# Two-layer ReLU² network behind block attention: where the block sums of the squares and of the weights are formed, in which order their products run, and how the softmax steps are laid between them

## The chip, the cores and the metric

One core of one Trainium2 chip runs the whole program. The metric is the time of one execution in microseconds; three executions of the kernel before gave a median of 700.97 us (700.53 to 701.24). Engines are named as in the profile: PE multiplies matrices, PEld loads its weights, DVE is VectorE, ACT is ScalarE, POOL is GpSimd, SP issues the DMAs.

## The reference

Attention over 4 batches, 8 heads, 768 positions and 64 channels gives 3072 rows of 512, which go through `h = relu(x @ w_in)` (512 to 2048) and `(h * h) @ w_out` (2048 to 512). In the attention, each query sees its neighbours within 15 positions and one summary of every block of 32 keys:

```python
k_sum = k.reshape(B, H, nb, block, D).max(axis=3)
v_sum = v.reshape(B, H, nb, block, D).mean(axis=3)
scores_l = scale * q @ k.T            # masked to |i - j| < 16
scores_s = scale * q @ k_sum.T + log(block)
a = softmax(concat(scores_l, scores_s))
attn = a @ concat(v, v_sum)
h = relu(x @ w_in)
out = (h * h) @ w_out
```

## The kernel before

The 3072 rows are 12 chunks of 256 rows (two groups of 128). Every operand of a large multiplication is split into a high and a low part, and three products (high·high, high·low, low·high) stand for one. Chunks 0 and 1 run in an opening stage that an order written out by hand sets (`START`), beside the loading and decoding of the weights. From chunk 2 on the program is a loop: chunk c has eight slots, and slot n handles the n-th pair p of the sixteen 128-wide blocks of the hidden layer. Nothing reorders it: each engine takes its instructions in the order in which the code issues them.

In slot n the PE runs the first layer of pair n (24 matmuls, L388), and then the second layer of the pair before it, n − 1. From chunk 3 on, for seven of the eight pairs, the second layer is not the plain 2 by 2 product of blocks (12 matmuls of 512 columns, L580) but seven products of sums of blocks (Strassen's way, 21 matmuls of 256 columns, L515). That needs sums of the blocks of the squares, for each slot, and sums of the weights' blocks, once for each pair.

The squares of a slot (`squares_and_sums`, L431): ACT takes the ReLU from the accumulator `ph` into `r` (L396) and the high part of the square of three plain blocks into `gh` (L402); DVE multiplies `ph` by `r` in place (L436) and subtracts for the plain low parts `gl` (L437); POOL forms four sums in place in `r`, each 128x128 (L439 to L442); then ACT rounds the four sums to their high parts (`split_sums`, L446) and POOL subtracts for their low parts (L447). `r` has two buffers, which alternate. The products (`products`, L505) go block by block: for every one of the seven, both uses of the high part and then the low part.

The sums of the weights (`build`, L474) have five steps: 0 and 1 add high and low parts of the two blocks' halves on POOL (L480), 2 and 3 are four subtractions on POOL (L483 to L488), and 4 rounds on ACT (L492, L493) and takes the low parts on DVE (L494, L495). The table `BUILDS` says in which slot of chunk 2 or 3 and at which place in it each step stands: steps 0 to 3 of a pair stand together at a slot's end, and step 4 ahead of the next slot's ReLU. Four of the seven pairs' sums are written to memory and streamed back in each chunk (`stream`).

Beside this, chunk c prepares the attention of the two groups a = 2c + 2 and a + 1 of the next chunk: scores on PE (L273, in slots 0 and 3), a masked maximum for each head on DVE (L300), the exponential on ACT (L308), the inverse of the sums on DVE (L318, L321), the normalizing on POOL (L326, four heads at a time), twelve 32-row transposes on DVE (L339, three, five and four in three places), and in slot 7 the weighted values on PE (L357), whose result is split on ACT and DVE (L370, L373) into the input of the next chunk. For the next batch's block summaries, half a key or value array at a time is loaded into the one buffer `kv_sb` (L188) and reduced on DVE (L191, L196); a load follows at a slot's end, and its reduction one slot later. `place_k` and `place_v` copy summaries to where the multiplications read them. `period` hands each slot its steps in three lists: "before" the squares, "after" them (but ahead of `split_sums`), and "last". In slot 0 the results of the chunk before are added up and stored (L544 to L556).

Of the kernel before, what the change touches and what calls it, by code (L numbers as in the profile page):

```python
# [76 lines left out]
def attn_ffn_kernel(ctx: ExitStack, tc: tile.TileContext, q, k, kt, v, vt, v0, w, masks, ident, mean, out):  # L77
# [346 lines left out]
    def squares(ph, k):  # L424

        r = relu(ph, r_sb[:, k], nc.scalar)
        high_square(flat(gh_sb, k), r)
        square(ph, r)
        low_square(flat(gl_sb, k), ph, flat(gh_sb, k))

    def squares_and_sums(ph, k):  # L431
# [5 lines left out]
        nc.vector.tensor_sub(out=gl_sb[:, k, o], in0=r[:, o], in1=gh_sb[:, k, o].bitcast(F32))  # L437
# [1 line left out]
        nc.gpsimd.tensor_sub(out=a11, in0=a11, in1=a21)  # L439
        nc.gpsimd.tensor_add(out=a21, in0=a21, in1=a22)  # L440
# [1 line left out]
        nc.gpsimd.tensor_sub(out=a12, in0=a12, in1=a22)  # L442

    def split_sums(k):
        o = slice(3 * P, 7 * P)
        nc.scalar.copy(out=gh_sb[:, k, o], in_=r_sb[:, k])  # L446
        nc.gpsimd.tensor_sub(out=gl_sb[:, k, o], in0=r_sb[:, k], in1=gh_sb[:, k, o].bitcast(F32))  # L447
# [26 lines left out]
    def build(p, step):  # L474
# [7 lines left out]
        if step == 2:  # L482
            nc.gpsimd.tensor_sub(out=t1, in0=t3, in1=t1)  # L483
# [21 lines left out]
    def products(p, k, closes):  # L505
# [4 lines left out]
        for blk, b, n_ps, o in (  # L510
            (2, b11, 2, lo), (0, b21, 6, lo), (1, t4, 7, lo),
            (5, t3, 3, lo), (6, t1, 3, hi), (4, t2, 2, hi), (3, b22, 6, hi),
        ):
            for n, (g_, w) in enumerate(((gh_sb, 0), (gh_sb, 1), (gl_sb, 0))):
                nc.tensor.matmul(  # L515
                    bank[n_ps][:, o], lhsT=g_[:, k, blk * P : (blk + 1) * P], rhs=b[:, w],
                    start=False, stop=(n == 2 and (n_ps, o.start) in closes),
                )
# [334 lines left out]
```

## Time and profile before

| what | value |
|---|---|
| median of three executions | 700.97 us |
| profiled execution, its own time | 701.86 us |
| its span, first to last instruction | 700.1 us |
| mean granted TensorE clock | 0.958 |
| PE busy (matmuls) | 620.0 us, 89% |
| DVE busy | 431.8 us, 62% |
| ACT busy | 293.1 us, 42% |
| POOL busy | 327.4 us, 47% |
| DMA, mean | 130 GB/s |

A matmul's end in the profile is modelled, so that PE counts as busy in nearly every stretch in which matmuls follow one another; the pace is better read from how many matmuls start in a stretch. "Granted clock" is the share of its full clock that the PE had. "idle before, releaser" in a row is the time that an engine stood idle ahead of its instructions, and the engine and line whose end released them. All of this is of the one profiled execution.

### The profile page before, as it was taken

The numbers are of one execution on the slowest core, as the hardware profiler recorded it, in microseconds if no ns is written. First come the engines' busy times: TensorE is split into PE (matmuls) and PEld (weight loads), VectorE is DVE, ScalarE is ACT, GpSimd is POOL, SyncE is SP. The second block draws the span as 40 slices with busy tenths as digits, with TensorE's granted clock in tenths as the row PEclk, the third lists the DMA queues.
The fourth block names the chain that finished last, engine by engine and source line by source line (L and its number), as shares of the span: only waits on it lengthen the run. The fifth ranks groups of instructions, "written<-read, shape, count | busy, mean of one in ns | idle before, by whom it ended". The sixth has DMA issues, their size and how long they took to land.

```text
span 700.1 us, 14848 instructions
## 1 busy us (share of the span) xinstructions
PE 620.0 (89%) x5859; PEld 576.2 (82%) x5859; DVE 431.8 (62%) x1112; ACT 293.1 (42%) x748; POOL 327.4 (47%) x441
## 2 busy tenths in 40 slices
...
GB/s 344 212 324 382 65 61 111 197 93 83 45 46 188 129 105 47 240 138 47 159 128 47 146 167 111 144 151 129 91 114 108 93 134 128 107 64 88 160 53 31
DMA packets 27638, 91.15 MB, mean 130 GB/s; under 512 B 3376, under 2 KB 3504, under 8 KB 25520
## 3 DMA queue, kind: packets, MB, share of 16 engines
...
q14 instruction: 24, 0.20, 0.1%
...
## 4 chain that ended last, share of the span: by engine, by line
PE 40%; DVE 18%; POOL 17%; ACT 15%; issue 4%; DMA 3%; SPq 0%; POOLq 0%; DVEq 0%; ACTq 0%
PE ph L388 16%; PE zw L515 7%; ACT e_sb L308 5%; PE o_ps L456 4%; POOL gl L447 3%; PE o_ps L515 3%; DVE r L436 3%; DVE gl L437 3%; ACT r L396 3%; ACT gh L402 3%; ACT gh L446 2%; DMA kv_sb<-in_kt 2%; POOL r L442 2%; POOL r L439 2%; POOL r L440 2%
## 5 line engine op out<-in xcount | busy, mean ns | idle before, releaser
L388 PE MATMUL ph<-xh,w_sb 128*128 128x256 f32 x1408 | 254.9, 283 | 1.4 <-DVE gl L410 1.1
L388 PEld LDWEIGHTS ph<-xh,w_sb 128*128 128x128 f32 x1408 | 219.1, 192 | 7.0 <-issue 3.0
L388 PE MATMUL ph<-xl,w_sb 128*128 128x256 f32 x704 | 198.0, 281 | 0.0
L388 PEld LDWEIGHTS ph<-xl,w_sb 128*128 128x128 f32 x704 | 134.7, 191 | 0.4 <-DVE xl L373 0.4
L308 ACT ACTIVATE e_sb<-e_sb,nmx 128x120 f32<-128x120 f32 x192 | 73.9, 386 | 90.3 <-DVE nmx L300 90.3
L446 ACT CAST gh<-r 128x512 fp32r<-128x512 f32 x63 | 39.1, 620 | 170.8 <-POOL r L442 163.7
L439 POOL TENSOR_TENSOR r<-r 128x128 f32<-128x128 f32 x63 | 29.0, 460 | 169.6 <-DVE sm L318 85.5
L436 DVE TENSOR_TENSOR r<-ph,r 128x512 f32<-128x512 f32 x63 | 43.6, 692 | 104.4 <-ACT gh L402 102.6
L339 DVE STREAM_TRANSPOSE pT<-e_sb 32x256 f32<-32x256 f32 x228 | 99.4, 436 | 5.9 <-POOL e_sb L326 2.6
L447 POOL TENSOR_TENSOR gl<-r,gh 128x512 fp32r<-128x512 f32 x63 | 80.7, 1281 | 32.9 <-ACT gh L446 32.9
L396 ACT ACTIVATE r<-ph 128x512 f32<-128x512 f32 x85 | 50.0, 588 | 44.7 <-PE ph L388 41.1
L326 POOL TENSOR_TENSOR e_sb<-e_sb,sm 128x480 f32<-128x480 f32 x43 | 44.2, 1027 | 42.6 <-DVE sm L321 19.2
L515 PE MATMUL zw<-sums,gl 128*128 128x256 f32 x126 | 40.4, 321 | 26.4 <-POOL gl L447 26.4
L402 ACT ACTIVATE gh<-r 128x384 fp32r<-128x384 f32 (+1 forms) x96 | 53.9, 561 | 20.5 <-PE o_ps L456 12.9
L515 PE MATMUL zw<-sums,gh 128*128 128x256 f32 x252 | 52.1, 289 | 8.2 <-ACT gh L446 8.0
L515 PE MATMUL zw<-w_sb,gh 128*128 128x256 f32 x252 | 52.3, 289 | 3.0 <-ACT gh L402 3.0
L580 PE MATMUL o_ps<-w_sb,gh 128*128 128x512 f32 x144 | 48.3, 419 | 6.8 <-ACT gh L402 6.8
L515 PEld LDWEIGHTS zw<-sums,gl 128*128 128x128 f32 x126 | 25.0, 198 | 33.2 <-POOL gl L447 33.2
L252 POOL TENSOR_TENSOR w_raw<-w_raw 128x1024 int32<-128x1024 int32 x16 | 34.2, 2145 | 37.3 <-ACT w_raw L243 12.5
L515 PE MATMUL o_ps<-w_sb,gh 128*128 128x256 f32 x252 | 51.0, 284 | 0.0
L515 PEld LDWEIGHTS zw<-sums,gh 128*128 128x128 f32 x252 | 39.8, 195 | 9.6 <-ACT gh L446 9.6
L300 DVE CUSTOM_DVE_ANT_0 e_sb<-s_ps,mask_sb 128x120 f32<-128x120 f32 x192 | 43.2, 274 | 6.3 <-PE s_ps L288 5.6
(120 smaller groups left out, 1211.2 us busy)
## 6 DMA issues: line engine op xcount, KB each, us to landing
sums<-sums SPq DMA_DIRECT2D x40, 768.0 KB, 4.4
...
v_sb<-in_v SPq DMA_DIRECT2D x24, 384.0 KB, 6.9
k_sb<-in_k SPq DMA_DIRECT2D x18, 384.0 KB, 5.1
...
kv<-in_kt SPq DMA_DIRECT2D x8, 384.0 KB, 3.3
kv_sb<-in_kt SPq DMA_DIRECT2D x8, 384.0 KB, 5.9
```

What stands on the lines that cost most here:

```text
L300: nc.vector.tensor_tensor_reduce(out=e_sb[:, h, 0:NK], in0=s_ps[g][h % 2][:, h // 2, 0:NK], in1=m, scale=-scale, scalar=3.0e38, op0=ALU.ad ...
L308: nc.scalar.activation(e, e, AF.Exp, bias=nmx[half][:, i : i + 1], scale=-1.0, accum_out=sm[half][:, i : i + 1])
L326: eng.tensor_mul(out=e, in0=e, in1=sm[half].unsqueeze(2).to_broadcast([P, 4, NK]))
L339: nc.vector.transpose(out=pT[g % 2][j * 32 : j * 32 + 32, :, i * 32 : i * 32 + 32], in_=e_sb[i * 32 : i * 32 + 32, :, j * 32 : j * 32 + 32],)
L388: nc.tensor.matmul(ph, lhsT=w_sb[f][:, w, cc * P : (cc + 1) * P], rhs=x[c][:, cc, :], start=(n == 0), stop=(n == 3 * NC4 - 1))
L396: nc.scalar.activation(r, ph, AF.Relu)
L402: nc.scalar.activation(gh, r, AF.Square)
L436: nc.vector.tensor_mul(out=r, in0=ph, in1=r)
L446: nc.scalar.copy(out=gh_sb[:, k, o], in_=r_sb[:, k])
L447: nc.gpsimd.tensor_sub(out=gl_sb[:, k, o], in0=r_sb[:, k], in1=gh_sb[:, k, o].bitcast(F32))
L515: nc.tensor.matmul(bank[n_ps][:, o], lhsT=g_[:, k, blk * P : (blk + 1) * P], rhs=b[:, w], start=False, stop=(n == 2 and (n_ps, o.start) in ...
L580: nc.tensor.matmul((X, Y)[tt], lhsT=g_[tt], rhs=w_sb[2 * p + i][:, w, DM:], start=(begins and i == 0 and m == 0), stop=(ends and i == 1 an ...
```

## The change

It has these parts.

1. `squares_and_sums`: the four sums move from POOL to DVE, into a tile of their own (`s`), with other signs; two of them are one instruction of 256 elements (one operand read twice), the other two follow, each needing the one before. The plain low parts (384 elements) move from DVE to POOL. `r` and `s` have one buffer each.
2. `products`: the three plain blocks come first with all three uses; then the four sums' blocks with their two uses of the high part; then the four uses of the low part.
3. `BUILDS`: the steps stand one or two at a place, over two slots for a pair; step 4 stands mostly behind the slot's squares. Signs follow part 1.
4. `period` and `slot`: a fourth list, "mid", between the squares and `split_sums`; "after" now comes behind `split_sums`. Four maxima stand together ahead of the squares, four exponentials, the inverse and the normalizing in "mid", the other four maxima and exponentials in "after"; the transposes are split six, two and four.
5. Loads of half key or value arrays have two slots instead of one until their reduction, and are spread over the chunk; the copies of `place_k` stand together in slot 7, and those of `place_v` one slot later.
6. `evict_products` and `evict_outputs` are one, and store the first half earlier.

The diff, cut to its core:

```diff
@@ BUILDS
-    2: [(p + 1, "last", p, step) for p in (1, 2, 3, 4, 5) for step in range(4)]
-    + [(p + 2, "before", p, 4) for p in (1, 2, 3, 4, 5)],
...
+    2: [(2, "a", 1, 0), (2, "a", 1, 1), (3, "b", 1, 2), (3, "b", 1, 3), (3, "a", 1, 4)]
+    + [(4, "b", 2, 0), (4, "b", 2, 1), (4, "a", 2, 2), (4, "a", 2, 3), (5, "b", 2, 4)]
...
@@ squares_and_sums
-        nc.vector.tensor_sub(out=gl_sb[:, k, o], in0=r[:, o], in1=gh_sb[:, k, o].bitcast(F32))
         a12, a22, a11, a21 = (r[:, i * P : (i + 1) * P] for i in range(4))
-        nc.gpsimd.tensor_sub(out=a11, in0=a11, in1=a21)
-        nc.gpsimd.tensor_add(out=a21, in0=a21, in1=a22)
-        nc.gpsimd.tensor_sub(out=a22, in0=a22, in1=a11)
-        nc.gpsimd.tensor_sub(out=a12, in0=a12, in1=a22)
+        s1, s3, s2, s4 = (s_sb[:, i * P : (i + 1) * P] for i in range(4))
+        nc.vector.tensor_sub(
+            out=s_sb[:, 0 : 2 * P].rearrange("p (a b) -> p a b", a=2), in0=a21.unsqueeze(1).to_broadcast([P, 2, P]),
+            in1=r[:, P : 3 * P].rearrange("p (a b) -> p a b", a=2),
+        )
+        nc.gpsimd.tensor_sub(out=gl_sb[:, k, o], in0=r[:, o], in1=gh_sb[:, k, o].bitcast(F32))
+        nc.vector.tensor_sub(out=s2, in0=a11, in1=s1)
+        nc.vector.tensor_sub(out=s4, in0=a12, in1=s2)
@@ products
-            for n, (g_, w) in enumerate(((gh_sb, 0), (gh_sb, 1), (gl_sb, 0))):
...
+        passes = [(m, n) for m in plain for n in range(3)] + [(m, n) for m in summed for n in range(2)]
+        for (blk, b, n_ps, o), n in passes + [(m, 2) for m in summed]:
@@ slot
-        for do in after:
+        for do in mid:
             do()
         if summed:
             split_sums(k)
+        for do in after:
+            do()
@@ period
-            before[n].append(lambda g=g: softmax(g, 0, 4))
-            after[n] += [lambda: inverse(0), lambda: norm(0, nc.gpsimd), lambda g=g: softmax(g, 4, 6)]
-            before[n + 1] += [lambda g=g: softmax(g, 6, 8), lambda: inverse(1), lambda: norm(1, nc.gpsimd)]
-            after[n + 1].append(lambda g=g: turn(g, 0, 3))
-            before[n + 2].append(lambda g=g: turn(g, 3, 8))
+            before[n].append(lambda g=g: [mask_max(g, h) for h in range(4)])
+            mid[n] += [lambda: [exponentials(h) for h in range(4)], lambda: inverse(0), lambda: norm(0, nc.gpsimd)]
+            after[n].append(lambda g=g: [mask_max(g, h) for h in range(4, 8)])
+            after[n].append(lambda: [exponentials(h) for h in range(4, 8)])
+            before[n + 1] += [lambda: inverse(1), lambda: norm(1, nc.gpsimd)]
+            after[n + 1].append(lambda g=g: turn(g, 0, 6))
+            before[n + 2].append(lambda g=g: turn(g, 6, 8))
...
-            for n, p in enumerate(((0, 1), (2, 3))[t // 4]):
-                last[2 * n].append(lambda p=p: load_half(b + 1, p, kt))
-                after[2 * n + 1].append(lambda p=p: sum_k(b + 1, p))
...
+            last[1].append(lambda: load_half(b + 1, p, kt))
+            after[3].append(lambda: sum_k(b + 1, p))
...
```

Line numbers of the changed kernel are four to eight higher than before. Three places show how the order on an engine moves.

On the DVE, before, from the second inverse of a chunk's second softmax (slot 5) to the last of its transposes (slot 6); `r` are the squares, `pT` the transposed probabilities:

```order
L318 SCALAR_TENSOR_TENSOR sm<-sm 128x4
L321 RECIPROCAL sm<-sm 128x4
L436 TENSOR_TENSOR r<-ph,r 128x512
L437 TENSOR_TENSOR gl<-r,gh 128x384
L339 STREAM_TRANSPOSE pT_77<-e_sb 32x8x32 x8
L436 TENSOR_TENSOR r<-ph,r 128x512
L437 TENSOR_TENSOR gl<-r,gh 128x384
L339 STREAM_TRANSPOSE pT_77<-e_sb 32x8x32 x4
```

The same place after the change, from the reciprocal on (`s` are the sums):

```order
L325 RECIPROCAL sm<-sm 128x4
L440 TENSOR_TENSOR r<-ph,r 128x512
L443 TENSOR_TENSOR s<-r 128x256
L448 TENSOR_TENSOR s<-r,s 128x128
L449 TENSOR_TENSOR s<-r,s 128x128
L343 STREAM_TRANSPOSE pT_77<-e_sb 32x8x32 x8
L440 TENSOR_TENSOR r<-ph,r 128x512
L443 TENSOR_TENSOR s<-r 128x256
L448 TENSOR_TENSOR s<-r,s 128x128
L449 TENSOR_TENSOR s<-r,s 128x128
L343 STREAM_TRANSPOSE pT_77<-e_sb 32x8x32 x4
```

In each slot one subtraction of 384 elements has given way to three instructions that form the sums; the transposes stand behind them.

On the PE, before, the last twelve of the 21 products of a slot, those of the blocks of sums (`gh` and `gl` are high and low parts; `zw` and `o_ps` the output banks; `sums` and `w_sb` the weights' side):

```order
L515 MATMUL zw<-sums,gh 128x256 x2
L515 MATMUL zw<-sums,gl 128x256
L515 MATMUL zw<-w_sb,gh 128x256 x2
L515 MATMUL zw<-w_sb,gl 128x256
L515 MATMUL zw<-sums,gh 128x256 x2
L515 MATMUL zw<-sums,gl 128x256
L515 MATMUL o_ps<-w_sb,gh 128x256 x2
L515 MATMUL o_ps<-w_sb,gl 128x256
```

The same twelve after the change:

```order
L522 MATMUL zw<-sums,gh 128x256 x2
L522 MATMUL zw<-w_sb,gh 128x256 x2
L522 MATMUL zw<-sums,gh 128x256 x2
L522 MATMUL o_ps<-w_sb,gh 128x256 x2
L522 MATMUL zw<-sums,gl 128x256
L522 MATMUL zw<-w_sb,gl 128x256
L522 MATMUL zw<-sums,gl 128x256
L522 MATMUL o_ps<-w_sb,gl 128x256
```

The sums' first low part is read by the 18th product instead of the 12th, and the first high part by the 10th as before.

On ACT, before, in slots 3 and 4 of chunk 2, where step 4 of two weights' sums stands (the casts to `sums` and `w_sb`):

```order
L492 CAST sums<-ob 128x768
L493 CAST w_sb<-ob 128x256
L396 ACTIVATE r<-ph 128x512
L402 ACTIVATE gh<-r 128x512
L492 CAST sums<-ob 128x768
L493 CAST w_sb<-ob 128x256
L308 ACTIVATE e_sb,sm<-e_sb,nmx 128x120 x4
L396 ACTIVATE r<-ph 128x512
L402 ACTIVATE gh<-r 128x512
```

After the change, from the squares of slot 3 to the second of these steps:

```order
L400 ACTIVATE r<-ph 128x512
L406 ACTIVATE gh<-r 128x512
L499 CAST sums<-ob 128x768
L500 CAST w_sb<-ob 128x256
L400 ACTIVATE r<-ph 128x512
L406 ACTIVATE gh<-r 128x512
L312 ACTIVATE e_sb,sm<-e_sb,nmx 128x120 x8
L499 CAST sums<-ob 128x768
L500 CAST w_sb<-ob 128x256
```

The ReLU and the square of slot 3 have moved ahead of the rounding of the first weights' sum. The second has moved from ahead of slot 4's ReLU to ahead of slot 5's, behind all eight exponentials.

More of the change, by code (lines that the diff above doesn't have):

```diff
@@ L39 @@
 BUILDS = {
-    2: [(p + 1, "last", p, step) for p in (1, 2, 3, 4, 5) for step in range(4)]
-    + [(p + 2, "before", p, 4) for p in (1, 2, 3, 4, 5)],
-    3: [(0, "last", 7, step) for step in range(4)] + [(1, "before", 7, 4)]
-    + [(step + 1, "after", 6, step) for step in range(4)] + [(5, "before", 6, 4)],
[7 rows of a table added]
 }
@@ L509, in products @@
         lo, hi = slice(0, CT), slice(CT, DM)
[L510 to L513, printed above, removed]
-            for n, (g_, w) in enumerate(((gh_sb, 0), (gh_sb, 1), (gl_sb, 0))):
[L515 to L518, printed above, removed]
+        plain = (2, b11, 2, lo), (0, b21, 6, lo), (1, t4, 7, lo)
+        summed = (4, t3, 3, lo), (3, t1, 3, hi), (5, t2, 2, hi), (6, b22, 6, hi)
+        passes = [(m, n) for m in plain for n in range(3)] + [(m, n) for m in summed for n in range(2)]
+        for (blk, b, n_ps, o), n in passes + [(m, 2) for m in summed]:
+            g_, w = ((gh_sb, 0), (gh_sb, 1), (gl_sb, 0))[n]
+            nc.tensor.matmul(
+                bank[n_ps][:, o], lhsT=g_[:, k, blk * P : (blk + 1) * P], rhs=b[:, w],
+                start=False, stop=(n == 2 and (n_ps, o.start) in closes),
+            )
     def open_banks(*banks):
@@ L583, in second, with slot @@
                     )
-    def slot(c, n, before, after, last):
+    def slot(c, n, before, mid, after, last):
         p, k = order(c)[n], n % 2
@@ L621, in period @@
     def period(c):
-        before, after, last = [[] for _ in range(8)], [[] for _ in range(8)], [[] for _ in range(8)]
+        before, mid, after, last = steps = [[[] for _ in range(8)] for _ in range(4)]
         for n, where, p, step in BUILDS.get(c, ()):
-            {"before": before, "after": after, "last": last}[where][n].append(lambda p=p, step=step: build(p, step))
+            steps["bmal".index(where)][n].append(lambda p=p, step=step: build(p, step))
         if c > 2:
@@ L639, in period @@
         if a >= n_g:
-            return before, after, last
+            return steps
+        if t == 0 and b:
+            after[1].append(lambda: sum_v(b, 3))
+            after[2] += [lambda: place_v(a), lambda: place_v(a + 1)]
+        elif t == 4 and b + 1 < B:
+            after[1].append(lambda: sum_v(b + 1, 1))
         if a > FROM_PAIRS:
             last[0] += [lambda: load_v(a), lambda: load_v(a + 1)]
-        if b and t == 0:
-            after[1] += [lambda: place_v(a), lambda: place_v(a + 1)]
@@ L652, in period @@
         if b + 1 < B and t:
[L653 to L657 removed]
+            p = t - 2
+            last[1].append(lambda: load_half(b + 1, p, kt))
+            after[3].append(lambda: sum_k(b + 1, p))
@@ L658, in period @@
+            last[3].append(lambda: load_half(b + 1, p, vt))
+            after[5].append(lambda: sum_v(b + 1, p))
+            last[5].append(lambda: load_half(b + 1, p + 1, kt))
+            after[7].append(lambda: sum_k(b + 1, p + 1))
+            last[7].append(lambda: load_half(b + 1, p + 1, vt))
         if a + 3 < n_g:
```

48 lines of the change are left out of this document (23 added, 25 removed), and 5 rows, old and new, of the table BUILDS.

## The prediction

> **What bounds the kernel now.** I read the page first, then the windows by chunk, the groups, the waits, and the timeline of slots that run late. The page says that the PE is the engine to watch:
>
> ```profile
> PE 620.0 (89%) x5859; PEld 576.2 (82%) x5859; DVE 431.8 (62%) x1112; ACT 293.1 (42%) x748; POOL 327.4 (47%) x441
> ```
>
> The next rows are the windows from the start of one chunk's first layer to the next: chunk 2, chunk 3 and so on to chunk 11. The columns are the stretch, its length, busy time and count of PE, PEld, DVE, ACT and POOL, the granted clock, and DMA.
>
> ```profile
> 140.97:207.09 66.12, 54.04 (x388) 46.82 (x385) 37.49 (x101) 22.93 (x62) 32.77 (x37) 0.90 0.20 70
> 207.09:272.41 65.32, 54.06 (x474) 50.09 (x473) 35.55 (x93) 23.90 (x64) 35.07 (x50) 0.90 0.38 126
> 272.41:328.23 55.82, 50.38 (x484) 47.51 (x482) 33.74 (x94) 21.46 (x60) 25.61 (x40) 0.97 0.40 133
> 328.23:381.56 53.33, 49.42 (x484) 47.26 (x483) 32.03 (x92) 21.15 (x60) 27.62 (x43) 0.97 0.33 110
> 381.56:437.43 55.87, 50.42 (x484) 47.54 (x482) 33.68 (x94) 21.47 (x60) 25.61 (x40) 0.97 0.41 133
> 437.43:494.06 56.63, 51.30 (x483) 48.44 (x482) 33.67 (x94) 21.47 (x60) 25.60 (x40) 0.94 0.40 131
> 494.06:547.34 53.28, 49.36 (x483) 47.21 (x482) 31.99 (x92) 21.14 (x60) 27.59 (x43) 0.97 0.34 109
> 547.34:597.79 50.45, 48.13 (x483) 45.96 (x482) 30.50 (x88) 21.27 (x60) 25.63 (x40) 1.00 0.35 116
> 597.79:648.34 50.55, 48.27 (x484) 46.09 (x483) 30.49 (x88) 20.78 (x58) 25.64 (x40) 1.00 0.28 90
> 648.34:700.06 51.72, 46.84 (x378) 44.99 (x376) 15.94 (x28) 14.44 (x26) 23.43 (x37) 0.99 0.22 82
> ```
>
> What would a chunk take if the PE never waited? These stretches hold, undisturbed: both groups' weighted values, a first layer, the 21 products, one group's scores, the opening of banks, and a plain second layer.
>
> ```profile
> 432.84:434.85 2.01, 2.01 (x65) 1.94 (x65) 0.67 (x1) 1.65 (x3) 0.98 (x1) 1.00 0.17 70
> 437.43:440.16 2.73, 2.73 (x26) 2.73 (x25) 0.00 (x0) 0.62 (x1) 1.55 (x2) 1.00 0.00 0
> 440.16:442.63 2.47, 2.47 (x23) 2.35 (x21) 1.39 (x2) 1.46 (x3) 0.00 (x0) 1.00 0.00 0
> 442.63:443.62 0.99, 0.99 (x34) 0.83 (x33) 0.78 (x2) 0.14 (x1) 0.00 (x0) 1.00 0.03 8
> 446.45:446.89 0.44, 0.44 (x5) 0.39 (x3) 0.23 (x4) 0.44 (x5) 0.00 (x0) 1.00 1.02 391
> 446.89:449.69 2.80, 2.80 (x14) 2.27 (x13) 0.80 (x2) 1.84 (x7) 0.00 (x0) 1.00 1.00 305
> ```
>
> A chunk with sums is 8 x 2.73 + 7 x 2.47 + 2.80 + 0.44 + 2 x 0.99 + 2.01 = 46.4 us; chunk 2, whose second layers are all plain and which has one set of scores, is 8 x (2.73 + 2.80) + 0.99 + 2.01 = 47.2. So chunks 2 and 3 lose 19 us each, chunks 4 to 8 (which load for the next batch) 7 to 10, chunks 9 and 10 about 4. The groups say to whom:
>
> ```profile
> L515 PE MATMUL zw<-sums,gl 128*128 128x256 f32 x126 | 40.4, 321 | 26.4 <-POOL gl L447 26.4
> L447 POOL TENSOR_TENSOR gl<-r,gh 128x512 fp32r<-128x512 f32 x63 | 80.7, 1281 | 32.9 <-ACT gh L446 32.9
> L439 POOL TENSOR_TENSOR r<-r 128x128 f32<-128x128 f32 x63 | 29.0, 460 | 169.6 <-DVE sm L318 85.5 <-DVE gl L437 70.1 <-ACT xh L370 14.1
> L440 POOL TENSOR_TENSOR r<-r 128x128 f32<-128x128 f32 x63 | 29.0, 460 | 4.9
> L446 ACT CAST gh<-r 128x512 fp32r<-128x512 f32 x63 | 39.1, 620 | 170.8 <-POOL r L442 163.7 <-DVE vsum L196 7.1
> L436 DVE TENSOR_TENSOR r<-ph,r 128x512 f32<-128x512 f32 x63 | 43.6, 692 | 104.4 <-ACT gh L402 102.6 <-PE ph L388 0.7
> L437 DVE TENSOR_TENSOR gl<-r,gh 128x384 fp32r<-128x384 f32 x63 | 36.7, 582 | 2.1
> L396 ACT ACTIVATE r<-ph 128x512 f32<-128x512 f32 x85 | 50.0, 588 | 44.7 <-PE ph L388 41.1 <-DVE zw L407 3.5
> L402 ACT ACTIVATE gh<-r 128x384 fp32r<-128x384 f32 (+1 forms) x96 | 53.9, 561 | 20.5 <-PE o_ps L456 12.9 <-DVE r L398 5.0
> L339 DVE STREAM_TRANSPOSE pT<-e_sb 32x256 f32<-32x256 f32 x228 | 99.4, 436 | 5.9 <-POOL e_sb L326 2.6
> L480 POOL TENSOR_TENSOR ob<-w_sb 128x512 f32<-128x512 f32 x14 | 18.0, 1300 | 16.6 <-DMA out<-ob 12.1 <-DVE w_sb L495 4.5
> L483 POOL TENSOR_TENSOR ob<-ob 128x256 f32<-128x256 f32 x7 | 5.1, 734 | 0.0
> L492 ACT CAST sums<-ob 128x768 fp32r<-128x768 f32 x7 | 5.8, 833 | 36.9 <-POOL ob L488 36.9
> L495 DVE TENSOR_TENSOR w_sb<-ob,w_sb 128x256 fp32r<-128x256 f32 x2 | 0.8, 415 | 0.0
> L191 DVE TENSOR_REDUCE ksum<-kv_sb 128x24 f32<-128x768 f32 x8 | 7.6, 953 | 14.8 <-DMA kv_sb<-in_kt 14.7
> L308 ACT ACTIVATE e_sb<-e_sb,nmx 128x120 f32<-128x120 f32 x192 | 73.9, 386 | 90.3 <-DVE nmx L300 90.3
> ```
>
> The PE's largest wait is for the sums' low parts on POOL. Three more chains feed it: ACT stands 36.9 us at L492 for the weights' sums, with the next ReLU queued behind; DVE stands 14.7 us at L191 for a load, with the next slot's multiply behind; and after a long wait the clock drops. Two windows around such a wait in chunk 6 show the last (here PE alone):
>
> ```profile
> 408.70:412.10 3.40, 3.36 (x30) 0.50 0.19 73
> 412.10:415.50 3.40, 3.40 (x45) 1.00 0.26 77
> ```
>
> 30 matmuls against 45 in the same time: such a window costs up to half of itself, 1.7 us.
>
> **Products and sums.** Take t = 0 at a slot's ReLU. Before: ReLU 0.59 and square 0.56, multiply from 1.2 to 1.9, low part 0.58 to 2.5, four POOL sums of 0.46, each 0.08 behind the last (L440's idle 4.9 over 63), to 4.7, rounding 0.62 to 5.35, low part 1.28 to 6.7. The PE meanwhile does 2.47 + 2.73, begun 0.2 ahead of the ReLU, and opens this slot's products at 5.0; the 12th of them wants the low part 1.3 later, at 6.3. The wait of 0.4 is what 26.4 us over 63 slots make. After: the paired sum costs 0.42 (L495, 256 elements), the single ones 0.25 each by the slope from 256 to 384 elements (L495 to L437): the sums end at 2.9 if nothing disturbs them. The plain low part on POOL is 1.0 (between L439's 0.46 for 128 and L447's 1.28 for 512). Does it disturb them? These rows say yes:
>
> ```profile
> 457.57 0.16 DVE L318 SCALAR_TENSOR_TENSOR sm<-sm 128x4 f32<-128x4 f32 x1 [0.73 <-ACT e_sb L308]
> 477.97 1.28 POOL L447 TENSOR_TENSOR gl<-r,gh 128x512 fp32r<-128x512 f32 x1
> 478.52 0.74 DVE L318 SCALAR_TENSOR_TENSOR sm<-sm 128x4 f32<-128x4 f32 x1 [1.54 <-ACT e_sb L308]
> ```
>
> The same small DVE instruction takes 0.16 alone, and 0.74 when POOL is in the middle of L447: it ends at 479.26, with POOL's at 479.25. So I let POOL's low part begin when the paired sum has ended, at 2.3, and hold off the two single sums until 3.3. They end at 3.9, the rounding at 4.5, the low part at 5.85. The PE now wants it as its 18th product, at 5.0 + 17 x 0.12 = 7.0, and the high part as its 10th, at 6.0. Nothing waits; without the hold-off the low part would be there at 4.8. The Trainium skill says the same (SBUF — State Buffer, § Who interferes with whom): a DVE instruction with two SBUF inputs and a GpSimd instruction that reads SBUF exclude each other for a whole instruction. By that rule the sum is the one I take; the trace agrees, 0.16 against 0.74.
>
> **The transposes come late.** The DVE now has 0.69 + 0.42 + 1.0 of holding off + 0.50 = 2.6 us a slot where it had 1.27. From slot 5's multiply to the last transpose that is 2 x 2.6 + 12 x 0.44 = 10.5 instead of 7.8. In slot 4 the exponentials of heads 4 to 7 wait for maxima that stand behind the sums' 3.9 and the inverse (I estimate from 4.5) and hold the ACT for 4 x 0.39 until 6.1, so slot 5's ReLU is 1.0 late and its multiply begins at 2.2: the last transpose ends at 12.7. The PE wants it for the second group's values after 2.47 + 2.73 + 2.47 + 2.73 + 1.0 - 0.2 = 11.2. A wait of 1.5 per chunk takes the place of those removed. Behind it the DVE still has slot 7's 2.6 and two subtractions like L436's 0.69 before the next chunk's input is there, the PE only 1.0 + 2.47: 0.5 more. Chunks 9 and 10 come to 46.4 + 2.0 = 48.4 each: together 4 us less than before.
>
> **Loads.** The page's rows of the issues give the time from issue to landing:
>
> ```profile
> sums<-sums SPq DMA_DIRECT2D x40, 768.0 KB, 4.4
> kv_sb<-in_kt SPq DMA_DIRECT2D x8, 384.0 KB, 5.9
> ```
>
> 5.9 is more than one slot of 5.2 and less than two, so the wait at L191 goes. On SP's queue each load waits for the reduction that frees the buffer; behind it stand the next stream of sums, which has two slots for its 4.4, and the stores, for which nothing waits at once. I take nothing for that. But in chunks 4 to 8 a reduction of 0.95 stands among the transposes and another ahead of a multiply; I count 1.15 (it, with its scaling) onto the transposes' wait and 1.0 for the other: 50.6 a chunk. Five of them had 274.9 and get 253.0, a gain of 21.9, from which I take two windows of low clock, 3.4: 18.5.
>
> **Weights' sums.** A pair holds POOL for 2 x 1.30 + 4 x 0.73 = 5.5 us, then ACT and DVE, and before all that lay between one slot's squares and the next one's. In the new order POOL has two slots for it, and ACT mostly rounds behind the squares, so chunk 2's slots run at 5.53. What is late then is again the transposes: from slot 5's multiply, two multiplies with low parts (2.8), two step 4 (by L495 and the slope 1.5 each) and 5.3 of transposes are 11.1, and they end at 12.3, 0.4 after the PE's 11.9 even if they never wait for POOL's pieces; with those I put 2.5, and one window of low clock, on 47.2. That is 51.4: a gain of 14.7. Chunk 3 has three pairs (16.5 us of POOL) beside seven slots with 2.3 and four normalizings of 1.0: 36.6 of 46.4 us, and every two-input DVE instruction meets it. Its bounds are chunk 4's 50.6 and today's 65.3. In slots 2 to 5 a piece of 2.6 to 2.9 of a pair stands on POOL ahead of the low parts, whose slack is 1.1: 4 x 1.6; the four steps at once in slot 0 I put at 2, the transposes' wait at the 3.2 of a loading chunk and 1.5 for a step 4 ahead of it, and one window of low clock: 46.4 + 6.4 + 2 + 4.7 + 1.7 = 61.2, a gain of 4. Chunk 11 has no softmax; it loses its seven waits of 0.4, and I leave 0.8 for the banks' opening: 2 us.
>
> The regrouped maxima and exponentials and the moved copies are the same instructions beside PE work, and I take nothing for them but the 1.0 above. In the merged eviction one add of 256 elements moves behind the first store; if that holds the opening of the banks, it is by 0.42 in nine chunks, 3.8 at most, and the earlier store can win nothing that somebody waits for.
>
> **The sum.** 14.7 + 4 + 18.5 + 4 + 2 = 43.2. The profiled execution's 701.86 becomes 658.7; the median before was 0.9 below it, so I say 658.
>
> **Rivals.** (1) No hold-off: the sums end at 2.9, the transposes 1.4 earlier and nearly in time. Chunks 4 to 10 then run at 46.5 to 46.9, which adds 21 + 4, chunk 3 adds 5: 73 in all, 628. Against it is the 0.74. Chance 0.15. (2) The clock: each chunk's wait for transposes takes windows below full clock. One in each of nine chunks is 9 x 1.7, of which I have counted four: 8.5 more, 666; two in each make 682; I put 674. For it: chunks 4 to 8, which lose 7 us and more, have 0.94 to 0.97 in the clock's column; against it: chunks 9 and 10, which lose 4, have 1.00. The Trainium skill (TensorE: Matmul & The Clock Gate, § What's actually happening) has the clock gated by free-running windows of 3.4 us; the trace's 408.7 to 412.1 agrees in length. By that rule a wait of 1.5 can fall across two windows and cost nothing. Chance 0.14. (3) The sums come no earlier in the softmax slots, because the DVE is behind throughout; only chunk 2 and the loads gain, 14.7 and some 10: 676. Chance 0.08. (4) Slower: POOL is ahead at each of the three sums in a slot, each waiting out a low part of 1.0 to 1.28. Then DVE has 5.2 a slot, and chunk 4's 33.7 becomes 33.7 - 8.9 + 36.4 = 61, more than the PE's 46.4: nine chunks at 61 against 493 before, less chunk 2's gain, make about 742. It decides from 4.5 us a slot, that is 2.9 of waiting where I count 1.0. Against it: DVE follows its own multiply at once (L437's idle time is 2.1 us over 63). Chance 0.03. My own case has 0.60.
>
> **Chances and range.** About 0.2% is what a measurement of this kernel can tell from no change. Only (4) is slower: faster 0.96, within it 0.01, slower 0.03. From 628 (rival 1) to 680 (rivals 2 and 3, with a few us more for chunk 3's bound) the range leaves out little more than (4).
>
> **What would show it.** Right: the PE's wait for L454 (L447 before) nearly gone, a new one at the weighted values in slot 7 for the DVE's transposes; single sums of 128 elements at 0.9 or more in the first and 0.3 in the second; chunk 2 near 50; no idle DVE at the key reduction. Wrong: single sums at 0.3 each (rival 1), more half-clock windows than now (2), PE waits for low parts above 10 us (3), DVE above 90% busy in chunks 4 to 10 (4).

## The result, and the profile after

The changed kernel takes 667.15 us, the median of four runs (666.35 to 667.85), against 700.75 beside it: a ratio of 0.952 (95% interval 0.950 to 0.954). The forecast was 658, within 628 to 680. The profiled execution has a span of 666.0 us where the kernel before had 700.1.

DVE is the engine that changed most, from 62% to 77%:

```profile
PE 609.5 (92%) x5859; PEld 567.6 (85%) x5859; DVE 510.1 (77%) x1240; ACT 291.6 (44%) x748; POOL 277.9 (42%) x252
```

The same windows as in the prediction, chunk 2 to chunk 11:

```profile
139.88:193.58 53.70, 49.99 (x388) 44.21 (x385) 36.29 (x100) 22.04 (x60) 27.55 (x31) 0.97 0.21 72
193.58:257.70 64.12, 54.74 (x474) 50.64 (x472) 47.76 (x108) 25.04 (x67) 37.61 (x36) 0.89 0.38 134
257.70:309.33 51.63, 48.36 (x483) 45.98 (x482) 41.03 (x107) 20.58 (x58) 18.70 (x17) 1.00 0.42 143
309.33:360.86 51.53, 49.54 (x481) 46.43 (x482) 41.52 (x110) 21.23 (x61) 21.95 (x21) 1.00 0.37 121
360.86:411.83 50.97, 48.18 (x481) 46.02 (x482) 40.57 (x106) 21.15 (x61) 19.95 (x18) 1.00 0.40 138
411.83:465.15 53.32, 50.02 (x481) 47.51 (x482) 43.63 (x110) 20.99 (x60) 21.23 (x19) 0.97 0.41 139
465.15:516.15 51.00, 48.91 (x483) 46.13 (x482) 40.25 (x109) 21.22 (x61) 20.68 (x21) 1.00 0.37 122
516.15:565.19 49.04, 47.90 (x482) 45.84 (x482) 38.63 (x103) 21.05 (x61) 19.98 (x18) 1.00 0.37 119
565.19:614.23 49.04, 47.92 (x481) 45.84 (x482) 38.63 (x103) 20.95 (x60) 20.00 (x18) 1.00 0.29 93
614.23:666.00 51.77, 46.37 (x376) 44.72 (x376) 25.41 (x43) 14.20 (x25) 17.41 (x15) 1.00 0.22 82
```

Chunk 2 gained 12.4 us, chunk 3 1.2, chunks 4 to 8 together 16.5 (274.9 to 258.45), 9 and 10 2.9, chunk 11 nothing, and the loop begins 1.1 earlier: 34.1. The groups that answer to those of before (line numbers are the changed kernel's; behind the first bar stand the busy time in us and the mean of one in ns, behind the second the engine's idle time just before, and what ended it):

```profile
L443 DVE TENSOR_TENSOR s<-r 128x256 f32<-128x256 f32 x63 | 75.4, 1197 | 6.5
L448 DVE TENSOR_TENSOR s<-r,s 128x128 f32<-128x128 f32 x63 | 21.7, 345 | 2.2
L449 DVE TENSOR_TENSOR s<-r,s 128x128 f32<-128x128 f32 x63 | 20.3, 322 | 2.1
L522 PE MATMUL zw<-sums,gl 128*128 128x256 f32 x126 | 35.3, 303 | 4.4 <-POOL gl L454 3.9
L361 PE MATMUL s_ps<-pT,v_sb 128*64 128x64 f32 x288 | 13.0, 238 | 14.8 <-DVE pT L343 14.8
L312 ACT ACTIVATE e_sb<-e_sb,nmx 128x120 f32<-128x120 f32 x192 | 73.5, 384 | 25.9 <-DVE nmx L304 25.9
L195 DVE TENSOR_REDUCE ksum<-kv_sb 128x24 f32<-128x768 f32 x8 | 7.6, 947 | 0.1
L499 ACT CAST sums<-ob 128x768 fp32r<-128x768 f32 x7 | 5.8, 833 | 12.1 <-POOL ob L495 12.1
```

The PE's wait for the sums' low part fell from 26.4 us to 3.9, and a new one of 14.8 for the DVE's transposes stands at the weighted values, 1.6 on average in each of nine chunks. The load's wait is gone. One row moved that the prediction made nothing of: ACT's idle time ahead of the exponentials, 90.3 before, is 25.9. And it is the paired sum, not the single ones, that is slow: 1.20 us for 256 elements. The timeline of one slot, and of one of the few that differ, shows why (start and duration in us, engine, line and operation, and in brackets the idle time before it):

```profile
618.85 0.69 DVE L440 TENSOR_TENSOR r<-ph,r 128x512 f32<-128x512 f32 x1 [4.17 <-ACT gh L406]
619.62 1.02 POOL L447 TENSOR_TENSOR gl<-r,gh 128x384 fp32r<-128x384 f32 x1 [4.07 <-DVE r L440]
619.65 1.27 DVE L443 TENSOR_TENSOR s<-r 128x256 f32<-128x256 f32 x1
...
491.29 0.42 DVE L443 TENSOR_TENSOR s<-r 128x256 f32<-128x256 f32 x1
491.33 1.25 POOL L447 TENSOR_TENSOR gl<-r,gh 128x384 fp32r<-128x384 f32 x1 [1.95 <-DVE r L440]
491.75 0.98 DVE L448 TENSOR_TENSOR s<-r,s 128x128 f32<-128x128 f32 x1
```

Both engines are released by the same multiply. POOL begins 0.03 us ahead, and the paired sum ends 0.28 after POOL does; so it is in 57 of the 63 slots, and there the paired sum takes 1.25 to 1.28 us. Where DVE is ahead by 0.04, the paired sum takes 0.42, POOL 1.25, and the next sum waits in turn.

### The profile page after: what moved, and what is told of

It reads as the page before. It is cut to its first block, busy times and chain, and to the rows that moved or that the text cites. A ratio compares the mean times of both kernels' runs of the same rounds, so it can differ in the third digit from the quotient of the medians.

```text
span 666.0 us, 14839 instructions
## 1 busy us (share of the span) xinstructions
PE 609.5 (92%) x5859; PEld 567.6 (85%) x5859; DVE 510.1 (77%) x1240; ACT 291.6 (44%) x748; POOL 277.9 (42%) x252
## 4 chain that ended last, share of the span: by engine, by line
PE 39%; DVE 38%; ACT 12%; issue 5%; POOL 4%; DMA 1%; DVEq 0%; SPq 0%; ACTq 0%; POOLq 0%
PE ph L392 17%; DVE pT L343 8%; DVE s L443 8%; PE zw L522 6%; ACT e_sb L312 5%; DVE r L440 4%; PE o_ps L463 4%; PE o_ps L522 4%; PE o_ps L586 3%; ACT r L400 2%; DVE s L448 2%; DVE s L449 2%; ACT gh L406 2%; DVE e_sb L304 2%; DVE w_sb L263 1%
## 5 line engine op out<-in xcount | busy, mean ns | idle before, releaser
L392 PE MATMUL ph<-xh,w_sb 128*128 128x256 f32 x1408 | 251.9, 281 | 2.0 <-DVE gl L414 1.1
L392 PEld LDWEIGHTS ph<-xh,w_sb 128*128 128x128 f32 x1408 | 215.9, 189 | 8.2 <-issue 2.7
L392 PEld LDWEIGHTS ph<-xl,w_sb 128*128 128x128 f32 x704 | 132.8, 189 | 1.6 <-DVE xl L377 1.6
L447 POOL TENSOR_TENSOR gl<-r,gh 128x384 fp32r<-128x384 f32 x63 | 64.5, 1024 | 150.4 <-DVE r L440 145.7
L453 ACT CAST gh<-s 128x512 fp32r<-128x512 f32 x63 | 39.1, 621 | 181.2 <-DVE s L449 171.6
L454 POOL TENSOR_TENSOR gl<-s,gh 128x512 fp32r<-128x512 f32 x63 | 81.9, 1300 | 76.2 <-issue 58.4
L312 ACT ACTIVATE e_sb<-e_sb,nmx 128x120 f32<-128x120 f32 x192 | 73.5, 384 | 25.9 <-DVE nmx L304 25.9
L443 DVE TENSOR_TENSOR s<-r 128x256 f32<-128x256 f32 x63 | 75.4, 1197 | 6.5
L586 PE MATMUL o_ps<-w_sb,gh 128*128 128x512 f32 x144 | 46.1, 402 | 0.2 <-ACT gh L406 0.2
L411 DVE TENSOR_TENSOR ph<-ph,r 128x512 f32<-128x512 f32 x25 | 17.4, 695 | 33.6 <-ACT r L400 33.3
## 6 DMA issues: line engine op xcount, KB each, us to landing
w_raw<-in_w SPq DMA_DIRECT2D x16, 1024.0 KB, 10.2
```

Of the source, the lines that this page charges most:

```text
L312: nc.scalar.activation(e, e, AF.Exp, bias=nmx[half][:, i : i + 1], scale=-1.0, accum_out=sm[half][:, i : i + 1])
L392: nc.tensor.matmul(ph, lhsT=w_sb[f][:, w, cc * P : (cc + 1) * P], rhs=x[c][:, cc, :], start=(n == 0), stop=(n == 3 * NC4 - 1))
L443: nc.vector.tensor_sub(out=s_sb[:, 0 : 2 * P].rearrange("p (a b) -> p a b", a=2), in0=a21.unsqueeze(1).to_broadcast([P, 2, P]), in1=r[:, P ...
L447: nc.gpsimd.tensor_sub(out=gl_sb[:, k, o], in0=r[:, o], in1=gh_sb[:, k, o].bitcast(F32))
L454: nc.gpsimd.tensor_sub(out=gl_sb[:, k, o], in0=s_sb, in1=gh_sb[:, k, o].bitcast(F32))
L586: nc.tensor.matmul((X, Y)[tt], lhsT=g_[tt], rhs=w_sb[2 * p + i][:, w, DM:], start=(begins and i == 0 and m == 0), stop=(ends and i == 1 an ...
```

## The experiments

Two theories had to be told apart. Mine, as it stood in the prediction: the sums on DVE and the new order of the products end the wait for low parts, shorter waits in chunks 4 to 8 come from the loads, the softmax layout is worth nothing, and the hold-off by POOL costs 1.5 to 2 us a chunk. The rival: the gain comes from another part, and the move of the sums is no gain. All results are ratios to the kernel before, run beside each; the changed kernel's is 0.952, and 0.01 of ratio is 7 us. The intervals reach 0.002 to 0.004 to either side, so differences below some 3 us are not told apart.

**1. The order alone, on the kernel before.**

```diff
-        for blk, b, n_ps, o in (
...
+        passes = [(m, n) for m in plain for n in range(3)] + [(m, n) for m in summed for n in range(2)]
+        for (blk, b, n_ps, o), n in passes + [(m, 2) for m in summed]:
```

> The kernel before with nothing but the new order of the products (plain blocks, then the sums' two uses of the high part, then the four uses of the low part). Theory (order and sums are two cures for one wait, the 26.4 us for the sums' low part): that part is ready at 6.7 us in a slot and is now wanted at 7.0 instead of 6.3, so the wait falls below 8 us, chunks 9 and 10 take 48 to 48.6 us, and the time is 676 to 686. Rival (the sums have to come earlier; 0.7 us of slack is not enough where softmax work delays them): the wait stays above 15 us and the time is 690 or more.

689.33 us, 0.985 (0.981 to 0.989): 11 us. The PE's waits (total, how many, the longest):

```profile
PE zw L515 <- POOL gl L447: 11.8, 26, 2.7
PE zw L515 <- ACT gh L446: 9.8, 15, 1.8
```

Between the two: of 26.4 us 11.8 stay, and the wait for the sums' high part (L446) is no shorter than the 8.0 us before, so the sums themselves come late.

**2. The order undone, in the changed kernel:**

```diff
-        for (blk, b, n_ps, o), n in passes + [(m, 2) for m in summed]:
...
+        for blk, b, n_ps, o in (
...
+            for n, (g_, w) in enumerate(((gh_sb, 0), (gh_sb, 1), (gl_sb, 0))):
```

> The changed kernel with the products back in the order of before, block by block. Theory (two cures for one wait): the low part, ready at 5.85 us in a slot, is wanted at 6.3, so little comes back: the wait for it stays below 10 us and the time is 667 to 674. Rival (the order carries the gain): the wait is above 15 us again and the time is 680 or more.

666.44 us, 0.951 (0.947 to 0.956): no difference. But the waits moved:

```profile
PE zw L522 <- POOL gl L454: 13.3, 17, 1.5
PE s_ps L361 <- DVE pT L343: 10.2, 9, 2.7
```

Low parts are waited for 13.3 instead of 3.9, above what the theory allowed, and transposes 10.2 instead of 14.8. My reading is that the DVE is what is behind in a chunk, and that waiting earlier for a low part shortens the wait for it in slot 7. It is not the whole account: the two waits together are 4.8 us longer, at no cost in time, and the granted clock of the profiled execution is higher, 0.982 against 0.974. In the changed kernel the order is worth nothing.

**3. The sums undone, in the changed kernel:** sums on POOL, plain low part on DVE, and with them the two buffers for `r`.

```diff
-        nc.vector.tensor_sub(
...
-        nc.gpsimd.tensor_sub(out=gl_sb[:, k, o], in0=r[:, o], in1=gh_sb[:, k, o].bitcast(F32))
...
+        nc.vector.tensor_sub(out=gl_sb[:, k, o], in0=r[:, o], in1=gh_sb[:, k, o].bitcast(F32))
+        nc.gpsimd.tensor_sub(out=a11, in0=a11, in1=a21)
...
```

> The changed kernel with the sums back on POOL and the plain low part back on DVE, everything else as changed. Theory (the sums on DVE cost what they bring: transposes late behind 2.55 us of DVE a slot): DVE has 1.27 us a slot again, the PE's 14.8 us of waiting for transposes fall below 5, the low part is just in time in the new order, and the time is 655 to 668, so not clearly slower than the changed kernel. Rival (the sums on DVE bring the gain): the wait for low parts is above 15 us, and the time is 675 or more.

661.26 us, 0.944 (0.941 to 0.948): 6 us faster than the change. The PE's waits:

```profile
PE zw L518 <- ACT gh L449: 9.9, 10, 1.8
PE s_ps L360 <- DVE pT L342: 3.0, 2, 2.7
PE zw L518 <- POOL gl L450: 2.9, 16, 0.3
```

The wait for transposes falls from 14.8 to 3.0, and the low part comes in time although the sums are on POOL again. The move to DVE, as it was made, costs time.

**4. One low part:** sums and plain blocks lie side by side (the fourth sum in the place of the fourth block, two buffers for the squares), POOL takes one low part of 896 elements behind the rounding, and the products use all low parts last. The softmax's maxima and sums share a tile there.

```diff
-        nc.gpsimd.tensor_sub(out=gl_sb[:, k, o], in0=r[:, o], in1=gh_sb[:, k, o].bitcast(F32))
...
-        nc.gpsimd.tensor_sub(out=gl_sb[:, k, o], in0=s_sb, in1=gh_sb[:, k, o].bitcast(F32))
+        rs = sr_sb[:, 4 * k * P : (4 * k + 7) * P]
...
+        nc.gpsimd.tensor_sub(out=gl_sb[:, k], in0=rs, in1=gh_sb[:, k].bitcast(F32))
```

> The changed kernel with one low part for plain blocks and sums together on POOL, taken behind the rounding of the sums, and all uses of low parts last. POOL then has nothing to do while DVE forms the sums. Theory (POOL's plain low part holds off the paired sum, and that makes the transposes late): the paired sum takes 0.42 us instead of 1.20, the sums' step 1.7 us instead of 2.55, the PE's wait for transposes falls from 14.8 us to below 4, and the time is 648 to 656. Rival (the paired sum is slow of itself, with an operand that is read twice, or the transposes are late for the exponentials and the normalizing): the paired sum stays near 1.2, or the wait for transposes above 9 us, and the time is 662 or more.

636.88 us, 0.910 (0.907 to 0.913): 30 us faster than the change, twice what was expected. The paired sum (L442 there), the wait for transposes, and chunks 4 and 10:

```profile
L442 DVE TENSOR_TENSOR sr<-sr 128x256 f32<-128x256 f32 x63 | 30.0, 477 | 7.3 <-POOL gl L453 1.4 <-DVE sr L439 0.5
```

```profile
PE s_ps L360 <- DVE pT L342: 4.0, 2, 2.6
```

```profile
252.83:300.23 47.40, 47.36 (x484) 45.80 (x483) 37.55 (x109) 21.18 (x62) 18.67 (x12) 1.00 0.46 156
536.92:584.15 47.23, 47.23 (x483) 45.79 (x482) 34.78 (x102) 21.41 (x62) 18.74 (x12) 1.00 0.31 96
```

0.48 instead of 1.20, so the operand read twice is not slow of itself, and every chunk from 4 to 10 is within some 1 us of the 46.4 that the PE needs.

**5. The plain low part on DVE, behind the sums**, and nothing else changed:

```diff
-        nc.gpsimd.tensor_sub(out=gl_sb[:, k, o], in0=r[:, o], in1=gh_sb[:, k, o].bitcast(F32))
         nc.vector.tensor_sub(out=s2, in0=a11, in1=s1)
         nc.vector.tensor_sub(out=s4, in0=a12, in1=s2)
+        nc.vector.tensor_sub(out=gl_sb[:, k, o], in0=r[:, o], in1=gh_sb[:, k, o].bitcast(F32))
```

> The changed kernel with the plain low part on DVE again, behind the sums, and nothing else changed. Theory (what costs is the time of DVE from a slot's multiply to the transposes behind it): the paired sum falls to 0.42 us, but 0.58 us for the low part come back, so a slot has 2.27 us on DVE instead of 2.55; of the 30 us that the kernel with one low part gained by taking 0.77 us from a slot, this gets a third: 653 to 660, chunks 9 and 10 at 48.2 to 48.6. Rival (that kernel gained by its two buffers for the squares and by the late uses of the low parts, not by DVE's time): 664 or more.

647.03 us, 0.921 (0.918 to 0.925): 22 of the 30 us. The paired sum, the transposes, and chunks 6 and 10:

```profile
L443 DVE TENSOR_TENSOR s<-r 128x256 f32<-128x256 f32 x63 | 27.8, 441 | 6.5
L343 DVE STREAM_TRANSPOSE pT<-e_sb 32x256 f32<-32x256 f32 x228 | 99.4, 436 | 3.3
```

```profile
352.54:400.99 48.45, 47.39 (x484) 45.70 (x482) 38.15 (x113) 21.46 (x60) 12.92 (x12) 1.00 0.44 145
545.99:593.12 47.13, 47.13 (x483) 45.62 (x482) 36.25 (x110) 21.04 (x58) 12.90 (x12) 1.00 0.31 96
```

DVE has more instructions, and the time is 22 us less; 18 of them are in chunks 4 to 10, where POOL has time to spare. So the hold-off costs at least that. Two other causes can be set aside: the one buffer for the squares is still there, and POOL's shorter queue does not bring the transposes forward, for their row is the same in the changed kernel, 3.3 us of idle time and no wait for POOL's normalizing. A third by DVE's time was too little; I take it that this is because the sums also end earlier, ahead of the rounding and its low part. Chunks 9 and 10 have nothing more to win, those with reductions still have 1 to 2. How the last 8 us of experiment 4 divide between DVE's time, the two buffers and the late low parts was not taken apart.

**6. The table of the weights' sums undone** ("l" is the list "last", "m" the list "mid"; before, the latter's place was called "after").

```diff
-    2: [(2, "a", 1, 0), (2, "a", 1, 1), (3, "b", 1, 2), (3, "b", 1, 3), (3, "a", 1, 4)]
...
+    2: [(p + 1, "l", p, step) for p in (1, 2, 3, 4, 5) for step in range(4)]
+    + [(p + 2, "b", p, 4) for p in (1, 2, 3, 4, 5)],
...
```

> The changed kernel with the table of before for the weights' sums (steps 0 to 3 at one place at a slot's end, step 4 ahead of the next ReLU). Theory (the spread pieces alone make chunk 2 shorter, and do something for chunk 3): chunk 2 back to 63 to 67 us, chunk 3 at 64 to 68, and the time is 676 to 684. Rival (chunk 2 gained by the new layout of the softmax): chunk 2 stays below 58 us, and the time is below 673.

679.70 us, 0.968 (0.964 to 0.971). Chunks 2 and 3:

```profile
139.95:206.91 66.96, 54.73 (x389) 46.94 (x385) 37.96 (x103) 22.77 (x62) 32.77 (x37) 0.90 0.19 68
206.91:269.69 62.78, 54.72 (x472) 50.30 (x473) 43.37 (x104) 23.61 (x64) 30.50 (x29) 0.92 0.37 126
```

All 13.3 us of chunk 2 are the table's. Chunk 3 is 1.3 shorter with the old one, which has pairs 4 and 5 done within chunk 2.

**7. The loads undone.**

```diff
-            last[1].append(lambda: load_half(b + 1, p, kt))
-            after[3].append(lambda: sum_k(b + 1, p))
...
+            for n, p in enumerate(((0, 1), (2, 3))[t // 4]):
+                last[2 * n].append(lambda p=p: load_half(b + 1, p, kt))
+                after[2 * n + 1].append(lambda p=p: sum_k(b + 1, p))
...
```

> The changed kernel with the loads of before: one slot from a load to its reduction, two pairs one behind the other in the first slots of a chunk. Theory (DVE's waits for loads go to the PE, since DVE is what is late in these chunks): three waits of some 4.8 us come back, in chunks 4, 6 and 7, which take 54 to 57 us, and the time is 673 to 682. Rival (DVE, 77% busy, makes such a wait up before the chunk ends): the waits come back and the time is 670 or less.

668.84 us, 0.952 (0.949 to 0.956): no difference, as the rival said. The waits came back, and chunk 6 is 3.5 longer, but chunk 5 1.2 shorter. Chunks 4 to 8 together are 3.1 longer, and chunk 2 is 2.8 shorter:

```profile
L195 DVE TENSOR_REDUCE ksum<-kv_sb 128x24 f32<-128x768 f32 x8 | 7.6, 952 | 11.5 <-DMA kv_sb<-in_kt 11.4
```

```profile
308.02:358.39 50.37, 48.71 (x482) 46.22 (x482) 39.87 (x107) 21.08 (x61) 21.67 (x21) 1.00 0.36 116
358.39:412.82 54.43, 49.74 (x481) 46.25 (x482) 42.41 (x109) 20.93 (x61) 20.09 (x18) 1.00 0.41 136
```

The spread gives to the chunks that waited and seems to take from those into which it moves a reduction; of chunk 2's 2.8 some 1.6 go with the granted clock, 1.00 here and 0.97 in the changed kernel.

**8. The softmax layout undone:** maxima and exponentials in turn, four heads ahead of the squares, two behind, two ahead of the next slot's squares.

```diff
+            before[n].append(lambda g=g: softmax(g, 0, 4))
+            mid[n] += [lambda: inverse(0), lambda: norm(0, nc.gpsimd), lambda g=g: softmax(g, 4, 6)]
+            before[n + 1] += [lambda g=g: softmax(g, 6, 8), lambda: inverse(1), lambda: norm(1, nc.gpsimd)]
+            mid[n + 1].append(lambda g=g: turn(g, 0, 3))
...
```

> The changed kernel with the softmax steps laid as before: maxima and exponentials in turn, four, two and two heads at a place, all ahead of the rounding of the sums, transposes three, five and four. Theory (the same instructions beside PE work, worth nothing by themselves): 664 to 671. Rival (maxima in fours are what lets ACT and POOL work without standing behind one another): 674 or more; or (maxima of heads 4 to 7 behind the sums are what makes the transposes late): 660 or less.

690.89 us, 0.983 (0.980 to 0.987): 22 us lost, where I had expected nothing. ACT's idle time ahead of the exponentials is far above the 25.9 of the changed kernel:

```profile
L312 ACT ACTIVATE e_sb<-e_sb,nmx 128x120 f32<-128x120 f32 x192 | 73.9, 386 | 112.8 <-DVE nmx L304 112.3
```

ACT and DVE in slot 1 of chunk 9, in which the first layer's last matmul begins at 540.58:

```profile
540.69 0.39 ACT L312 ACTIVATE e_sb<-e_sb,nmx 128x120 f32<-128x120 f32 x1 [3.46 <-DVE nmx L304]
...
541.85 0.38 ACT L312 ACTIVATE e_sb<-e_sb,nmx 128x120 f32<-128x120 f32 x1
...
542.23 0.57 ACT L400 ACTIVATE r<-ph 128x512 f32<-128x512 f32 x1
542.83 0.53 ACT L406 ACTIVATE gh<-r 128x384 fp32r<-128x384 f32 x1
543.45 0.69 DVE L440 TENSOR_TENSOR r<-ph,r 128x512 f32<-128x512 f32 x1 [2.18 <-issue]
```

The ReLU stands behind four exponentials, which stand behind maxima, which stand behind the DVE's additions of the results. DVE waits 2.18 us, till 0.09 after the square's end, for its multiply (the row names no releaser). In the changed kernel that slot's ReLU begins 0.37 us after the last matmul has begun, here 1.65. The second softmax of a chunk is hit harder: on average over chunks 4 to 10 this delay is 4.2 us in slot 4 and 5.2 in slot 5, against 0.7 and 2.2 in the changed kernel.

**9. Only the exponentials put back ahead of the ReLU.**

```diff
+            before[n] += [lambda g=g: [mask_max(g, h) for h in range(4)], lambda: [exponentials(h) for h in range(4)]]
+            mid[n] += [lambda: inverse(0), lambda: norm(0, nc.gpsimd)]
...
+            before[n + 1] += [lambda: [exponentials(h) for h in range(4, 8)], lambda: inverse(1), lambda: norm(1, nc.gpsimd)]
```

> The changed kernel with one thing of the softmax layout put back: the exponentials of heads 0 to 3 stand ahead of the ReLU of their slot, those of heads 4 to 7 ahead of the ReLU of the next; maxima, transposes and all else as changed. Theory (the new layout is worth its 24 us because no ReLU stands behind exponentials that wait for maxima any more): most of it is lost, 680 to 692. Rival (the layout gained by grouping the maxima, by standing behind the rounding of the sums, or by the split of the transposes): 665 to 673.

694.77 us, 0.991 (0.989 to 0.994): all of the layout's worth is lost, and some 5 us more. The edit moves less than was meant. On ACT the exponentials of heads 4 to 7 already stood ahead of the next slot's ReLU in the changed kernel, so what moves there is those of heads 0 to 3, ahead of one ReLU and square, 18 times (and once, in chunk 2, the rounding of a weights' sum). DVE and POOL have the same order as before the edit. The ReLU's delay is 4.3 us in slot 4 and 4.7 in slot 5, close to experiment 8's. So four exponentials that stand ahead of a ReLU while they wait for their maxima carry the layout's worth in this kernel. ACT's idle time grows from 25.9 us:

```profile
L312 ACT ACTIVATE e_sb<-e_sb,nmx 128x120 f32<-128x120 f32 x192 | 73.6, 385 | 65.6 <-DVE nmx L304 65.6
```

**10. The layout alone, on the kernel before.**

```diff
-            before[n].append(lambda g=g: softmax(g, 0, 4))
...
+            before[n].append(lambda g=g: [mask_max(g, h) for h in range(4)])
+            mid[n] += [lambda: [exponentials(h) for h in range(4)], lambda: inverse(0), lambda: norm(0, nc.gpsimd)]
...
```

> The kernel before with nothing but the new layout of the softmax (the lists of the slot with it); loads, copies and the weights' sums keep their places. Theory (the layout frees the ReLU whatever engine forms the sums): 680 to 690, chunks 9 and 10 at 48 to 49.3 us. Rival (it is worth so much only beside sums on DVE, where DVE has no time left to wait for the ReLU): 694 or more.

695.70 us, 0.993 (0.991 to 0.995): 5 us, so the rival holds by the time; that it is for lack of time on DVE is not shown by this. The gain lies in chunks 2 and 3, which are 2.8 and 5.3 shorter; chunks 4 to 8 are together 2.6 longer. ACT's idle time ahead of the exponentials falls from 90.3 us to 24.5 all the same. In the kernel before, the ReLU's delay was only 0.45 us in slot 4 and 1.3 in slot 5, so there was little to free in those two. The PE still waits for the low part, with the exponentials now ahead of the rounding:

```profile
PE zw L515 <- POOL gl L447: 21.9, 27, 2.0
```

**11. The old layout in the kernel with one low part** (experiment 8's edit).

> The kernel with one low part, with the softmax steps laid as in the kernel before. Theory (the layout is worth what it is because of the ReLU, hold-off or not): 654 to 664. Rival (DVE with 0.77 us a slot to spare makes the late ReLU up): 646 or less.

662.62 us, 0.946 (0.944 to 0.948): 25 us lost, about as many as with the hold-off (22). The layout's worth does not come from the hold-off.

**12. Pair 6's weights' sums a chunk later,** in the kernel with one low part.

```diff
-    + [(4, "b", 6, 0), (4, "b", 6, 1), (5, "b", 6, 2), (5, "b", 6, 3), (5, "a", 6, 4)],
+    4: [(0, "a", 6, 0), (0, "a", 6, 1), (3, "b", 6, 2), (3, "b", 6, 3), (3, "a", 6, 4)],
...
-        summed = c > 2 and p > 0
+        summed = c > 2 and p > 0 and not (c == 3 and p == 6)
```

> The kernel with one low part, and the weights' sums of pair 6 formed in chunk 4 instead of chunk 3, where pair 6 runs its plain second layer once more (0.33 us longer by 2.80 against 2.47). Theory (chunk 3's 61 us are POOL's pieces standing ahead of the low parts, three pairs of them): chunk 3 falls to 55 to 58.5, chunk 4 stays below 49, and the time is 632 to 635.5. Rival (chunk 3 is long for other reasons, or chunk 4 pays the same): chunks 3 and 4 together as long as before, and 636 or more.

639.10 us, 0.911 (0.909 to 0.914), the same as without. Chunk 3 without it, then chunks 3 and 4 with it:

```profile
191.86:252.83 60.97, 50.83 (x474) 47.18 (x473) 46.26 (x108) 26.86 (x73) 34.88 (x30) 0.97 0.40 141
```

```profile
194.50:250.24 55.74, 50.41 (x464) 46.80 (x463) 42.03 (x104) 24.27 (x68) 27.48 (x22) 0.97 0.44 154
250.24:303.90 53.66, 49.64 (x482) 47.47 (x481) 41.81 (x111) 22.44 (x64) 24.01 (x18) 0.97 0.42 138
```

Chunk 3 falls by 5.2, and chunk 4 rises by 6.3: such a pair costs 5 to 6 us in either chunk, among slots with sums.

## Why the prediction was right, and where it was not

The sum came out near, 34 us in the profile for 43, and by chunks nearly in the shape that was forecast. Its causes were partly wrong, and that it came near is partly luck. For most chunks the prediction added up what would be left over the PE's own time and took every other wait as gone, so it did not need to know what takes the waits away. It put 18.5 us under the loads, which are worth nothing in time, and nothing under the layout, which is worth 22.

- **Weights' sums:** right for chunk 2, which gained 12.4 for 14.7, and the table is what brings it (experiment 6). Chunk 3 gained 1.2 for 4. The term that was too small is the clock: at 0.89 it loses some 7 of the chunk's 64.1 us, where one window of 1.7 was counted, while the PE's waits there come to 9.4 us for the 13.1 counted. The chunk's length goes with the pairs formed in it (experiment 12).
- **Hold-off:** its size was right, its place wrong. The step "I let POOL's low part begin when the paired sum has ended" failed: POOL begins with it, in 57 of 63 slots just ahead. 0.69 + 1.20 + 0.35 + 0.32 = 2.56 us a slot stand against the 2.6 forecast, and the wait for transposes is 1.6 a chunk for 1.5. The size came right because DVE waits out that one POOL instruction once in a slot either way, with the paired sum and not with the single ones. By its own sign, "single sums at 0.3 each (rival 1)", the prediction would have taken 0.35 and 0.32 for no hold-off at all. The 1.0 by which slot 5's ReLU was to be late is 1.8 on average over chunks 4 to 10 (2.2 after the last matmul, for 0.4 where nothing stands ahead of it). The Trainium skill (SBUF — State Buffer, § Who interferes with whom) also says "Issue order, not op shape, decides who blocks"; the two pieces of timeline above agree, and that sentence bears on this step.
- **Products and sums:** the step "Nothing waits" nearly came true (26.4 to 3.9), but as the cause of a gain it failed. The order is worth 11 us on the kernel before (experiment 1) and nothing in the changed kernel (2), and the sums on DVE cost 6 us (3). Without the hold-off the sums on DVE gain 14 us (5), or 24 with one low part and two buffers as well (4). Rival 1 was wrong about the hold-off, but not far off in what its absence is worth: it said 628, and these kernels take 647 and 637.
- **"The regrouped maxima and exponentials ... I take nothing":** this step failed most. The layout is worth 22 us here (8), through the ReLU that no longer stands behind the exponentials of heads 0 to 3 (9). The row was quoted: ACT's 90.3 us at L308, with the ReLU behind it on the same queue. I followed DVE's idle time and the PE's, and not ACT's. It is worth 5 us on the kernel before (10): what it brings depends on the rest, and the 90.3 us alone would not have given the 22.
- **Loads:** the wait at L191 went, as forecast, but the 21.9 us of chunks 4 to 8 are not the loads', which make 3.1 there (7); by experiment 8 the layout makes 3.7 in each, on average (these five take 276.8 us with the old one, 258.45 with the new).
- **Chunk 11:** the 2 us failed. The mean of 0.4 over all slots was counted, but by the waits before, chunk 11 had only this:

```profile
PE zw L515 <- POOL gl L447: 1.0, 3, 0.4
```

and after the change it pays more for the opening of the banks, whose additions stand behind the held-off sums:

```profile
PE o_ps L531 <- DVE ob L560: 1.5, 2, 0.9
```

- **Clock:** chunks 4 to 10 lost one window's worth (0.97 in chunk 7) where two were counted. Rivals 2 to 4 did not come.

Undone one at a time, the parts make 11 (table), 22 (layout), 0 (order), 0 (loads) and -6 us (sums): 27 of the 33.6. How the rest divides between what parts do together, the eviction and the copies of `place_k` was not measured.
